# Low parts of the weights by TensorE, T~ of 64 tokens, two halves of attention by turns, and x in two buffers

## The chip, the core and the metric

The kernel runs on one core of one Trainium2 chip. The metric is device time of one execution in microseconds. Before the change it is 740.63 us, the median of three runs (740.49 to 740.67).

## The reference

Four batches of eight heads with 768 tokens and 48 columns a head go through a delta rule, and its output, 3072 rows of 384, through a layer of 2048 columns with the Mish function. The weights come as float64.

```python
k_n = k / (np.linalg.norm(k, axis=-1, keepdims=True) + 1e-06)
for t in range(S):
    kt, vt, bt = (k_n[:, :, t], v[:, :, t], beta[:, :, t, None])
    y[:, :, t] = np.einsum('bhd,bhde->bhe', q[:, :, t], state)
    v_old = np.einsum('bhde,bhd->bhe', state, kt)
    state = state + bt[:, :, :, None] * np.einsum('bhd,bhe->bhde', kt, vt - v_old)
...
h = x @ w_in
sp = np.where(h > 20.0, h, np.log1p(np.exp(np.minimum(h, 20.0))))
g = h * np.tanh(sp)
return (g @ w_out).astype(np.float32)
```

## The kernel before

**Chunks.** The tokens are taken in twelve chunks of 64. With G the strictly lower part of K K^T, V' the scaled values and b' the scaled beta, a chunk has Z = (I + G b')^-1 (V' − K S), Z~ = b' Z, S <- S + K^T Z~ and Y = Q S + lower(Q K^T) Z~. The matrix T~ = b' (I + G b')^-1 depends on no state, so it is made ahead, for a group of two chunks at a time (`early`, L205): two pg products a chunk (L235) give the Gram blocks, DVE turns them so that each partition holds one 32 x 32 block, and a forward substitution of 30 steps of two operations (L290, L295) inverts them. Each chunk has two blocks of 32 to a head, c = 0 and c = 1, so T~ is known only inside a block. For group 0 the substitution runs on blocks of 16, with 14 steps, and `merge` (L310) adds the missing quarter by products ma and mb on PE (L321, L333). For group 1 GpSimd takes steps 1 to 17. The first block's T~ parts end in the tile tu (L304) and tt (L301).

**A chunk's attention** (`step`, L355) works on four pieces, one batch each, tile `xx` holding for each head Z~, Q^T with the masked products of Q and K, and K or the identity, beside S. A piece has 8 products in each of five stages: gq (L381, K S and K Q^T), za (L398, Z~ of the first 32 tokens), pr (L413, what these do to the next 32, which DVE subtracts from `vt` in L419), zb (L398, the next 32) and py with ps (L431, L437, Y and the new S). ACT copies za, zb, py and ps out of PSUM. The stages of different batches are staggered, and 20 such steps a chunk are spread over the layer's pieces of the chunk before. All of attention's PSUM tiles share four banks (pool `pa`, tag "at").

**The layer** (`moe`, L487) takes the 256 rows of one chunk, turned by xt (L481) into x, high and low part (L483, L484), one buffer each. Float32 accuracy comes from three float32r products: high by high, high by low, low by high. Eight times: `h` (L505, 18 products of 256 columns into one of two PSUM buffers), ACT Exp (L509), DVE (L510), ACT Square, Ln, Exp (L511 to L513), DVE (L514, the tile e), ACT copies the high part of g (L522), DVE, or GpSimd in the first three chunks, subtracts for the low part (L525). Two `h` later `acc` (L535, 12 products of 384 columns) adds to the output tile.

**The weights** (`convert`, L171) come in 12 parts of w_in, 128 x 512 (tiles mi, wi), and 16 of w_out, 128 x 384 (mo, wo). A part is made float32 from the two words of float64: ACT's Abs (L179), DVE's clamp (L180), shift (L182), sign (L187) and low word (L189). For the first four parts ACT and GpSimd make the sign instead (L193). Then ACT copies the high part (L198) and GpSimd subtracts it for the low part (L199). Twelve of the parts are loaded among the other first loads, the rest from about one and a half chunks' time before the first layer on.

**Order.** Every piece of work is given a time in units of a chunk (`put`), and pieces are emitted in that order; the order on each engine is then a scheduler's, except that DVE keeps the order of what passes `queue` (L158). Products of zeros, `keep_warm` (L567), follow some attention products at the start.

Of the kernel before, what the change touches and what calls it, by code (L numbers as in the profile page):

```python
# [1 line left out]

# [31 lines left out]
def kernel(  # L34
# [36 lines left out]
    PB = NP // B  # L71
# [283 lines left out]
    def step(n, y):  # L355
# [8 lines left out]
        def s1(b, half=None):  # L364
# [3 lines left out]
            if n:  # L368
                scale_v(b)
# [369 lines left out]
```

## Time and profile before

| | |
|---|---|
| median of the runs | 740.63 us |
| span of the profiled execution | 745.6 us |
| instructions | 22768 |
| TensorE busy (PE) | 682.3 us, 92% of the span |
| VectorE (DVE) | 534.3 us, 72% |
| ScalarE (ACT) | 468.9 us, 63% |
| GpSimd (POOL) | 127.4 us, 17% |
| chain that ended last | PE 67%, DVE 20% |

The times of the runs are measured without the profiler, the span with it; the profiled execution's own time is its span. PE is a product's time, PEld the loading of its stationary operand, which runs beside other products. In a group's row stand the line, the engine, the operation, the tiles it writes and reads, shapes and count, then the busy time, the mean time of one in ns, and the engine's idle time just before, with what ended it. In a timeline's row stand start, duration, engine, line, operation, tiles, shapes, count, and the idle time before. A product of float32 has two records, one of float32r one.

### The profile page before, as it was taken

How to read it: one execution, taken by the hardware profiler on the slowest of the kernel's cores; microseconds unless marked ns; L12 is line 12 of the kernel's file. 1: busy time of each engine (PE TensorE's matmuls, PEld its weight loads, DVE VectorE, ACT ScalarE, POOL GpSimd, SP SyncE). 2: the span in 40 equal slices, each digit the busy share in tenths (PEclk: the TensorE clock that was granted, in tenths of full speed). 3: DMA queues.
4: the chain of work that ended last, by engine and by line, in shares of the span. 5: the costliest groups of instructions: out<-in, count | busy, mean ns of one | idle time of the engine just before them, and what ended most of it. 6: DMA issues, size and time to landing. Idle time of an engine off the chain costs nothing.

```text
span 745.6 us, 22768 instructions
## 1 busy us (share of the span) xinstructions
PE 682.3 (92%) x9656; PEld 602.3 (81%) x9674; DVE 534.3 (72%) x1152; ACT 468.9 (63%) x1005; POOL 127.4 (17%) x171
## 2 busy tenths in 40 slices
PE   5659699878799989999999999999999999999993
PEld 3236588768788878998898998998988989989993
DVE  5796999997747997659995579975499964454351
ACT  2233667755485666776776767767767767767681
POOL 3431336894221221000000000000000000000000
PEclk9756999789899999999999999999999999999998
DMA  5762910253213032122222221130130120000000
GB/s 87 185 181 40 380 32 7 30 84 60 25 32 59 8 54 48 21 44 50 37 34 41 40 38 34 24 51 15 24 59 14 33 49 18 18 23 1 17 7 21
DMA packets 160981, 37.75 MB, mean 51 GB/s; under 512 B 154224, under 2 KB 157296, under 8 KB 160880
## 3 DMA queue, kind: packets, MB, share of 16 engines
q1 hardware_dynamic: 160880, 36.30, 24.0%
q8 instruction: 76, 1.25, 0.7%
q14 instruction: 25, 0.20, 0.1%
HBM read 31.56 MB, written 4.72 MB: 49 GB/s over the span
## 4 chain that ended last, share of the span: by engine, by line
PE 67%; DVE 20%; SPq 4%; issue 3%; ACT 2%; DMA 2%; POOL 1%; DVEq 0%; POOLq 0%; ACTq 0%
PE h L505 24%; PE acc L535 22%; PE gq L381 4%; SPq L131 3%; PE py L431 3%; PE pg L235 2%; PE za L398 2%; DVE pr L290 2%; PE zb L398 2%; PE pr L413 2%; DVE gt L295 2%; PE warm L570 2%; PE ps L437 2%; DVE e L514 1%; DVE xx L389 1%
## 5 line engine op out<-in xcount | busy, mean ns | idle before, releaser
L505 PE MATMUL h<-x,wi 128*128 128x256 f32 x1728 | 238.3, 291 | 13.5 <-DVE e L514 12.1
L505 PEld LDWEIGHTS h<-x,wi 128*128 128x128 f32 x1728 | 218.4, 192 | 23.8 <-DVE e L514 12.5
L535 PE MATMUL acc<-wo,g 128*128 128x384 f32 x1152 | 233.4, 350 | 2.3 <-ACT g L522 1.9
L535 PEld LDWEIGHTS acc<-wo,g 128*128 128x128 f32 x1152 | 201.1, 192 | 8.8 <-ACT g L522 2.5
L514 DVE SCALAR_TENSOR_TENSOR e<-e,h 128x512 f32<-128x512 f32 x96 | 65.8, 685 | 45.5 <-ACT e L513 43.9
L522 ACT CAST g<-e 128x512 fp32r<-128x512 f32 x96 | 59.3, 618 | 49.6 <-DVE e L514 48.6
L361 POOL TENSOR_TENSOR vt<-vt,ne 128x192 f32<-128x192 f32 x48 | 27.3, 589 | 351.9 <-DMA vt<-in_v_dram 187.1
L509 ACT ACTIVATE e<-h 128x512 f32<-128x512 f32 x96 | 57.2, 596 | 47.9 <-PE h L505 45.2
L511 ACT ACTIVATE e<-e 128x512 f32<-128x512 f32 x96 | 60.5, 631 | 33.0 <-DVE e L510 32.5
L510 DVE TENSOR_SCALAR e<-e 128x512 f32<-128x512 f32 x96 | 42.7, 446 | 32.2 <-ACT e L509 31.0
L525 DVE TENSOR_TENSOR g<-e,g 128x512 fp32r<-128x512 f32 x72 | 49.1, 681 | 19.2 <-ACT g L522 18.6
L512 ACT ACTIVATE e<-e 128x512 f32<-128x512 f32 x96 | 60.5, 632 | 2.7
L513 ACT ACTIVATE e<-e 128x512 f32<-128x512 f32 x96 | 60.4, 631 | 2.4
L419 DVE TENSOR_TENSOR vt<-vt,pr 32x192 f32<-32x192 f32 x96 | 34.0, 354 | 32.7 <-PE pr L413 30.9
L290 DVE TENSOR_TENSOR pr<-gt 128x228 f32<-128x228 f32 (+14 forms) x147 | 53.9, 367 | 3.6 <-PE warm L292 0.5
L295 DVE TENSOR_TENSOR gt<-gt,pr 128x228 f32<-128x228 f32 (+14 forms) x147 | 51.5, 350 | 3.3
L372 DVE STREAM_TRANSPOSE xx<-qsrc 64x256 f32<-64x256 f32 x96 | 41.6, 437 | 13.9 <-PE ps L437 9.3
L381 PE MATMUL gq<-xx,kt 64*64 64x112 f32 (+1 forms) x768 | 47.6, 265 | 1.0 <-DVE x L484 1.0
L431 PEld LDWEIGHTS py<-xx 128*64 128x64 f32 x768 | 38.5, 138 | 10.7 <-issue 4.9
L431 PE MATMUL py<-xx 128*64 128x48 f32 x768 | 45.7, 227 | 1.0 <-ACT xx L403 0.3
L525 POOL TENSOR_TENSOR g<-e,g 128x512 fp32r<-128x512 f32 x24 | 31.9, 1328 | 74.1 <-ACT g L522 47.3
L381 PEld LDWEIGHTS gq<-xx,kt 64*64 64x64 f32 x768 | 37.4, 138 | 8.4 <-issue 4.5
(94 smaller groups left out, 838.3 us busy)
## 6 DMA issues: line engine op xcount, KB each, us to landing
ri<-in_moe_w_in_dram SPq DMA_DIRECT2D x12, 512.0 KB
ro<-in_moe_w_out_dram SPq DMA_DIRECT2D x16, 384.0 KB
vt<-in_v_dram SPq DMA_DIRECT2D x48, 96.0 KB
xx<-in_k_dram SPq DMA_DIRECT2D x96, 48.0 KB
out_dram<-o SPq DMA_DIRECT2D x24, 192.0 KB
qsrc<-in_q_dram SPq DMA_DIRECT2D x48, 64.0 KB
ksrc<-in_k_dram SPq DMA_DIRECT2D x44, 64.0 KB
qsrc<-in_q_dram SPq DMA_DIRECT2D x48, 32.0 KB
```

The lines of the kernel that those rows point to most:

```text
L290: queue(eng.tensor_tensor(out=pv, in0=nj, in1=xj, op=ALU.mult), on)
L295: queue(eng.tensor_tensor(out=below, in0=below, in1=pv, op=ALU.add), on)
L381: m = nc.tensor.matmul(ps[64 * hh:64 * hh + 64, p, :], kt[r, PB * b + p], x[r, p, hh, D - d:D + C], start=True, stop=True)
L431: nc.tensor.matmul(py[64 * hh:64 * hh + 64, p, :], x[:, p, hh, D:D + C], x[:, p, hh, 0:D], start=True, stop=True)
L505: nc.tensor.matmul(h[:, f2, :], wt["i", f * P // WI * NCH + c][:, i2, f0:f0 + P], x[:, c, :], start=(i == 0), stop=(i == 3 * NCH - 1))
L511: nc.scalar.activation(e, e, AF.Square)
L512: nc.scalar.activation(e, e, AF.Ln, bias=0.5, scale=0.5)
L513: nc.scalar.activation(e, e, AF.Exp, scale=-1.0)
L514: nc.vector.scalar_tensor_tensor(e, e, -1.0, h, op0=ALU.add, op1=ALU.mult)
L522: nc.scalar.copy(out=gg[:, 0], in_=e)
L525: eng.tensor_tensor(out=gg[:, 1], in0=e, in1=gg[:, 0], op=ALU.subtract)
L535: nc.tensor.matmul(acc[t], gg[:, a, f2, ts_], wt["o", f][:, i2, :], start=(f == 0 and i == 0), stop=(f == NF - 1 and i == 2))
```

## The change

The same numbers are computed, with this done in another way:

- **Halves.** A pair of heads that shares instructions is now (batch b, batch b+2), so a chunk's attention has two halves of 8 pairs instead of four pieces of 4, and `xx` two tiles.
- **T~ of 64 tokens.** The tile tt2 has 64 columns. After the blocks of 32 are done, ta = (masked K K^T of the two blocks) T~ and tb = T~ ta (functions s_a and s_b, 32 products of 32 columns each) fill the square between them. GpSimd copies the upper diagonal block beside it (move_diagonal), and DVE makes tn, the turned T~, that tb needs. Then one product of 64 rows a head, pz, gives all of Z~: za, pr, the subtraction and zb are gone.
- **By turns.** `together` emits the products of two stages alternately: pz of half 0 with gq of half 1, pz of half 1 with gq of the next chunk's half 0, tb of one chunk with ta of the next. gq is two tiles of four pairs a half. A half's py and ps stand alone. So a chunk's attention stands at four places in the layer.
- **Group 1** is split in 16s too, with merges 2 and 3; GpSimd's steps of the substitution are gone.
- **Weights.** Signs are all made by DVE. The low part of the first 22 parts is had on PE: a product with the identity of the float32 weight, plus one of its high part, into a tile lo of the attention's banks, which ACT copies with a minus sign. The stored number a is the weight's negative, so the high part is copied with a minus sign too. The last six low parts are DVE's. All parts are asked for at the start, among the other loads. 22 of the 28 parts have their conversion ahead of the first layer's `h`.
- **Order.** From t = −0.05 on (just ahead of the first `h`) PE keeps the order in which things are emitted. `h` and `acc` of all chunks form one sequence, so the next chunk's first two `h` stand before this chunk's last two `acc`. x has two buffers, and the turn of x stands before the last `h` of the chunk before. The last chunk's g takes a buffer of tn as well.
- **Keep-warm.** Behind each half of a merge stand 4 units of 128 columns instead of 18; behind each of chunk 0's other stages, 8.

```diff
-    PB = NP // B
+    PB = NP // 2
...
-    xx = [cp.tile([P, PB, 2, W], F32, name=f"xx{i}") for i in range(B)]
+    xx = [cp.tile([P, PB, 2, W], F32, name=f"xx{i}") for i in range(2)]
...
+    tt2 = cp.tile([P, 2, NP, C], F32, name="tt2")
...
-        if not rest:
-            sg = high.bitcast(F32)
-            nc.scalar.activation(sg, sg, AF.Sign, scale=-1.0)
-            nc.gpsimd.tensor_tensor(out=a, in0=a, in1=sg, op=ALU.mult)
...
-            nc.scalar.copy(out=w[:, 0], in_=a)
-        nc.gpsimd.tensor_tensor(out=w[:, 1], in0=a, in1=w[:, 0], op=ALU.subtract)
+        nc.scalar.mul(out=w[:, 0], in_=a, mul=-1.0)
+        if parts.index((kind, i)) < TN['pl']:
+            ps = pa.tile([P, 512], F32, tag="at", name=f"lo{kind}{i}")[:, :n]
+            nc.tensor.matmul(ps, ident, a, start=True, stop=False)
+            nc.tensor.matmul(ps, ident, w[:, 0].bitcast(F32), start=False, stop=True)
+            nc.scalar.mul(out=w[:, 1], in_=ps, mul=-1.0)
+            queue(nc.vector.scalar_tensor_tensor(w[:, 1], a, -1.0, w[:, 0], op0=ALU.mult, op1=ALU.subtract))
...
+    def move_diagonal(t2):
+        for hh in range(2):
+            r = slice(64 * hh, 64 * hh + 32)
+            nc.gpsimd.tensor_copy(out=tt2[r, t2, :, 0:32], in_=tt2[r, t2, :, 32:])
...
+    def together(*stages):
+        for step in zip_longest(*stages):
+            for f in step:
+                if f is not None:
+                    f()
...
+    def s_a(n):
+        at, tt = ats[n], tt2[:, n % 2]
+        ps = pa.tile([P, NP, 32], F32, tag="at", name=f"ta{n}")
...
+                r = slice(64 * hh + 32, 64 * hh + 64)
+                yield mm(ps[64 * hh:64 * hh + 32, p, :], at[r, p, :], tt[r, p, 32:],
+                         then=out if p == NP - 1 and hh else None)
...
+    def s_z(n, h):
+        vt, x, tt = vts[n, h], xx[h], tt2[:, n % 2]
+        pz = pa.tile([P, PB, D], F32, tag="at", name=f"pz{n}_{h}")
...
+                yield mm(pz[r, p, :], tt[r, PB * h + p, :], vt[r, p, :], then=out if p == PB - 1 and hh else None)
...
-        xs = [mp.tile([P, NCH, UT], F32R, tag=f"x{i}", name=f"x{i}_{n}", bufs=1) for i in range(2)]
+        xs = [mp.tile([P, NCH, UT], F32R, tag=f"x{i}", name=f"x{i}_{n}", bufs=2) for i in range(2)]
...
+    for n in range(1, NS):
+        t = n - 1.1 / NFP
+        put(one(turn, n), 1, t, t)
...
+        at(ts[0], (s_z, n, 0), (s_gq, n, 1))
+        at(ts[1], (s_y, n, 0))
+        at(ts[2], (s_z, n, 1), (s_gq, n + 1, 0))
+        at(ts[3], (s_y, n, 1))
...
+        at(t0 + u[0], (s_a, n))
+        at(t0 + u[1], (s_b, n), (s_a, n + 1))
+        at(t0 + u[2], (s_b, n + 1))
...
-    m0, m1 = TN.get('m', (9, 9))
+    m0, m1 = TN['m0'], 99
```

How this moves PE's instructions in a steady chunk. Before, in the layer of chunk 6 between two of its pieces (`x2` is that many alike in a row; a name's second number is the chunk's piece or batch, its last a buffer's): py and ps of one batch end, an `acc` follows, then zb of one batch, pr of the next.

```order
L437 MATMUL ps_0_6692<-xx_98 48x48 x2
L431 MATMUL py_0_6691<-xx_98 64x48 x2
L437 MATMUL ps_0_6692<-xx_98 48x48 x2
L535 MATMUL acc_6_6389<-wo_1102,g_2_6521 128x384 x3
L535 MATMUL acc_6_6389<-wo_1203,g_2_6521 128x384 x3
L535 MATMUL acc_6_6390<-wo_1102,g_2_6521 128x384 x3
L535 MATMUL acc_6_6390<-wo_1203,g_2_6521 128x384 x3
L398 MATMUL zb_1_6730<-vt_0_6192,tt_5497 32x48 x8
L413 MATMUL pr_2_6744<-xx_100,at_4402 32x48 x8
L505 MATMUL h_5_6755<-x_6_6280,wi_1462 128x256
```

Each stage of a batch is a piece of its own, zb and pr of neighbours standing together. Now, in the layer of chunk 5, the first rows of the place behind its fifth `h`: pz of half 1 and gq of the next chunk's half 0, one product of each in turn.

```order
L528 MATMUL h_4_6058<-x_5_5558,wi_1322 128x256
L393 MATMUL pz_1_6089<-vt_1_5024,tt_106 64x48
L393 MATMUL gq_00_6093<-xx_98,kt_4292 64x112
L393 MATMUL pz_1_6089<-vt_1_5024,tt_106 64x48
L393 MATMUL gq_00_6093<-xx_98,kt_4292 64x112
L393 MATMUL pz_1_6089<-vt_1_5024,tt_106 64x48
L393 MATMUL gq_00_6093<-xx_98,kt_4292 64x112
```

The two stages that stood at places of their own, with layer pieces between, are now one piece of 32 products, and its tiles are of one size.

The start on PE, now: merge 0 with low parts of w_out beside it.

```order
L335 MATMUL ma_0_572<-tu_564,d_156 32x16 x32
L583 LDWEIGHTS zero
L583 MATMUL warm<-zero 128x512
L335 MATMUL ma_1_608<-tu_564,d_156 32x16 x32
L583 LDWEIGHTS zero
L583 MATMUL warm<-zero 128x512
L199 MATMUL loo_646<-mo_568,ident 128x384
L200 MATMUL loo_646<-wo_644,ident 128x384
L199 MATMUL loo_658<-mo_650,ident 128x384
L347 MATMUL mb_0_667<-tt_106,ym_566 32x16 x14
L200 MATMUL loo_658<-wo_656,ident 128x384
L347 MATMUL mb_0_667<-tt_106,ym_566 32x16 x18
```

Before, the place holds ma and mb with five warm products behind each half and no low part. On GpSimd, before, behind the scaling of v (L361):

```order
L361 TENSOR_TENSOR vt_1_327<-vt_1_327,ne_397 128x192 x2
L193 TENSOR_TENSOR mi_402<-mi_402,ri_151 128x512
L199 TENSOR_TENSOR wi_418<-mi_402,wi_418 128x512
L193 TENSOR_TENSOR mi_473<-mi_473,ri_330 128x512
L199 TENSOR_TENSOR wi_490<-mi_473,wi_490 128x512
```

And now at the same place:

```order
L374 TENSOR_TENSOR vt_1_322<-vt_1_322,ne_420 128x384
L313 MEMSET ym_566 128x32x16
L323 COPY tt_106<-tt_106 32x16x32 x2
L374 TENSOR_TENSOR vt_0_976<-vt_0_976,ne_420 128x384
L374 TENSOR_TENSOR vt_1_979<-vt_1_979,ne_420 128x384
```

The conversion has left GpSimd; four short copies of diagonal blocks a group have come.

More of the change, by code (lines that the diff above doesn't have):

```diff
@@ new lines, in mm, with run, out @@
+    def mm(*a, then=None):
+        def run():
+            last[:] = [nc.tensor.matmul(*a, start=True, stop=True)]
+            if then is not None:
+                then()
+        return run
+    def s_a(n):
+        at, tt = ats[n], tt2[:, n % 2]
+        ps = pa.tile([P, NP, 32], F32, tag="at", name=f"ta{n}")
+        def out():
+            for hh in range(2):
+                r = slice(64 * hh, 64 * hh + 32)
+                nc.scalar.mul(out=at[r], in_=ps[r], mul=-1.0)
+        for p in range(NP):
+            for hh in range(2):
+                r = slice(64 * hh + 32, 64 * hh + 64)
+                yield mm(ps[64 * hh:64 * hh + 32, p, :], at[r, p, :], tt[r, p, 32:],
+                         then=out if p == NP - 1 and hh else None)
@@ new lines, in s_b, with out @@
+    def s_b(n):
+        at, tt, tn = ats[n], tt2[:, n % 2], tns[n // 2]
+        ps = pa.tile([P, NP, 32], F32, tag="at", name=f"tb{n}")
+        def out():
+            for hh in range(2):
+                r = slice(64 * hh, 64 * hh + 32)
+                nc.scalar.copy(out=tt[r, :, 32:], in_=ps[r])
+        for p in range(NP):
+            for hh in range(2):
+                r = slice(64 * hh, 64 * hh + 32)
+                yield mm(ps[r, p, :], tn[r, n % 2, p, :], at[r, p, :], then=out if p == NP - 1 and hh else None)
@@ L642, with at, run @@
     put(one(loads, TN.get('d1', ["q", "v", 2, "k2", 2, "k3", 2, "x", 22])), 1, -2.901, -2.901)
-    put(attend0, 1, -2.3, -2.3)
+    def at(t, *stages, warm=0):
+        def run():
+            together(*(f(*a) for f, *a in stages if a[0] < NS))
+            keep_warm(warm, last[-1])
+            yield
+        put(run(), 1, t, t)
+    put(one(lambda: [scale_v(0, h) for h in range(2)]), 1, -2.3, -2.3)
     put(one(loads, TN.get('d2', [28])), 1, TN.get('p1', -1.2) + 0.001, TN.get('p1', -1.2) + 0.001)
@@ L673 @@
             put(gen, 1, t, t)
[L674 to L685 removed]
+    units = [moe(n) for n in range(NS)]
@@ new lines @@
+    todo1 = [(n, fp) for n in range(NS) for fp in range(NFP)]
+    todo2 = list(todo1)
+    t = 0.0
+    lag = 2
+    for k, (n, fp) in enumerate(todo1):
+        t = n + (fp + 0.25) / NFP
+        put(one(units[n][0], fp), 1, t, t)
+        if n == NS - 1 and fp == 2:
+            lag = 3
+        elif k >= lag:
+            m, fq = todo2.pop(0)
+            t = n + (fp + 0.75) / NFP
+            put(one(units[m][1], fq), 1, t, t)
+    for i, (m, fq) in enumerate(todo2):
+        put(one(units[m][1], fq), 1, NS + i, NS + i)
```

322 lines of the change are left out of this document (132 added, 190 removed).

## The prediction

> **What bounds the kernel now.** I read the profile in this order: the page's head and slices, then busy time by stage (the span cut where the first `h` starts and where each chunk's output copies end), then groups of instructions, then single stretches of the timeline. The page first: the span, the granted clock in 40 slices, and the costliest group.
>
> ```profile
> span 745.6 us, 22768 instructions
> ...
> PEclk9756999789899999999999999999999999999998
> ...
> L505 PE MATMUL h<-x,wi 128*128 128x256 f32 x1728 | 238.3, 291 | 13.5 <-DVE e L514 12.1
> ```
>
> The profiled execution's 745.6 us stand 5.0 above the median of 740.63; I sum against 745.6 and take 5.0 off at the end. A slice is 18.6 us: the clock is under .9 in the first eleven slices only. By stage (the start from T~0's merges to the first `h`; chunk 0; 1; 2; 3 and 4; 9; 10; 11; the tail):
>
> ```profile
> core 0: us, PE busy (x) PEld busy (x) DVE busy (x) ACT busy (x) POOL busy (x), PEclk, DMA share, GB/s
> 44.00:93.10 49.10, 40.66 (x948) 27.25 (x959) 39.72 (x77) 21.04 (x56) 14.48 (x15) 0.71 0.64 215
> 93.10:176.10 83.00, 72.14 (x994) 65.06 (x993) 79.99 (x144) 54.44 (x117) 55.77 (x65) 0.89 0.27 40
> 176.10:228.40 52.30, 46.12 (x718) 42.66 (x717) 28.08 (x59) 32.24 (x74) 11.49 (x10) 0.93 0.22 38
> 228.40:288.00 59.60, 55.10 (x741) 48.34 (x743) 55.59 (x123) 36.56 (x81) 13.95 (x15) 1.00 0.24 39
> 288.00:392.80 104.80, 104.53 (x1526) 94.97 (x1526) 81.62 (x191) 73.37 (x159) 4.22 (x9) 1.00 0.24 40
> 602.20:651.40 49.20, 49.20 (x614) 44.86 (x612) 24.01 (x50) 35.65 (x76) 0.97 (x2) 1.00 0.14 27
> 651.40:700.50 49.10, 49.10 (x571) 44.55 (x570) 22.93 (x47) 33.91 (x70) 0.00 (x0) 1.00 0.03 9
> 700.50:734.30 33.80, 33.72 (x240) 33.40 (x238) 14.19 (x24) 24.05 (x43) 0.00 (x0) 1.00 0.04 13
> 734.30:745.60 11.30, 0.00 (x0) 0.00 (x0) 0.00 (x0) 0.45 (x1) 0.00 (x0) 0.73 0.10 35
> ```
>
> Chunk 0 is DVE's: 79.99 busy of 83.0. From 288 on PE never rests (104.53 of 104.8), so there only fewer or better packed products help. Chunks 1 and 2 lie between, PE idle 6.2 + 4.5 = 10.7. The last chunk has no attention beside it and gives the layer's bare price, by the groups in 700.5 to 734.3:
>
> ```profile
> L505 PE MATMUL h<-x,wi 128*128 128x256 f32 x144 | 17.8, 281 | 0.0
> L535 PE MATMUL acc<-wo,g 128*128 128x384 f32 x96 | 17.3, 334 | 0.0
> ```
>
> A chunk's layer is 33.8, an `h` 17.8 / 8 = 2.23, its products .124 each.
>
> **A steady chunk, part by part.** The pieces of attention as they stand between layer pieces, PE alone (records of a piece overlap, so a piece lasts from its start to the next one's):
>
> ```profile
> 517.54 0.98 PE L381 MATMUL gq<-xx,kt 64*64 64x112 f32 x16
> 518.46 2.41 PE L505 MATMUL h<-x,wi 128*128 128x256 f32 x18
> 520.80 0.32 PE L431 MATMUL py<-xx 128*64 128x48 f32 x4
> ...
> 521.76 2.38 PE L535 MATMUL acc<-wo,g 128*128 128x384 f32 x12
> 524.07 0.40 PE L398 MATMUL zb<-vt,tt 32*32 32x48 f32 x10
> ...
> 524.74 2.40 PE L505 MATMUL h<-x,wi 128*128 128x256 f32 x18
> 527.06 1.10 PE L235 MATMUL pg<-kt 64*32 64x64 f32 x64
> 528.09 0.53 PE L398 MATMUL za<-vt,tt 32*32 32x48 f32 x16
> 528.55 1.32 PE L535 MATMUL acc<-wo,g 128*128 128x384 f32 x6
> ```
>
> One batch: gq .92 (8 products, two records each), py with ps .96, za .46, zb with pr of another batch by turns .67, where apart they would be twice .46. Four batches: 3.68 + 3.84 + 1.84 + 2.68 = 12.04; two pg 2.06; layer 33.8. Chunks 3 and 4 took 104.8 / 2 = 52.4, so 4.5 is left for the transposes of x and for going from layer to attention and back at some 18 places. With .6 to .8 put to the transposes, about .21 a place.
>
> Now the change. Half a chunk has 16 gq products (1.84) and 16 pz by turns. Below: pz wholly inside gq, 1.84. Above: one after the other at za's price, 2.76, though a pz has 64 rows. By turns zb and pr take .67 / .92 = .73 of their sum, which gives 2.0; I take 2.1, nearest to that row. A chunk: 4.2 for gq, za, pr and zb together, before 8.2: −4.0. py and ps are the same products. New are ta and tb, 32 products of 32 columns each a chunk. By zb and pr's row, 16 products of 48 columns in .67, both are 1.34 × 2 × 32/48 = 1.8; alone at za's price 3.7; at best, with four tiles of 32 rows abreast all along, a quarter of that, .9. I take 1.8. The places fall from 18 to about 5.5 (four pieces, and ta, tb, pg, transposes mostly at the same places): −12.5 × .21 = −2.6. Sum −4.8: 47.6. DVE's and ACT's answers now come in fewer, larger lumps, an evicted piece being a whole half; I put .9 for it, and x's second buffer lets the next layer's first two `h` start before the last `acc`, which hides the turn of chunks. **48.5 a chunk**, 2.1 less where no pg is left.
>
> On DVE the subtractions behind pr go; the transposes for tn come. Both are off the path while PE is full.
>
> **The start.** T~0's merges start here, waiting for DVE, at half clock:
>
> ```profile
> 43.86 1.05 PE L321 MATMUL ma<-tu,d 16*32 16x16 f32 x64 [6.22 <-DVE tu L304]
> ```
>
> What GpSimd did to DVE in chunk 0, in rows of the timeline, of the groups in 93.1 to 176.1 and, for the least/median/longest, of the whole run; and GpSimd's own rows:
>
> ```profile
> 79.57 1.45 POOL L199 TENSOR_TENSOR wi<-mi,wi 128x512 fp32r<-128x512 f32 x1 [0.24 <-ACT wi L198]
> 79.83 1.46 DVE L182 TENSOR_SCALAR mi<-mi 128x512 int32<-128x512 int32 x1
> ```
> ```profile
> L187 DVE SCALAR_TENSOR_TENSOR mo<-ro,mo 128x384 int32<-128x384 int32 x9 | 9.0, 995 | 0.2
> L187 DVE SCALAR_TENSOR_TENSOR mi<-ri,mi 128x512 int32<-128x512 int32 x6 | 6.7, 1116 | 0.2
> L189 DVE SCALAR_TENSOR_TENSOR mo<-ro,mo 128x384 int32<-128x384 int32 x10 | 6.3, 633 | 0.2
> L189 DVE SCALAR_TENSOR_TENSOR mi<-ri,mi 128x512 int32<-128x512 int32 x6 | 5.4, 896 | 0.1
> ```
> ```profile
> L187 DVE SCALAR_TENSOR_TENSOR mo<-ro,mo x15: 508/830/1526, 46.6 to 170.2; 128x384 int32<-128x384 int32 x15
> L187 DVE SCALAR_TENSOR_TENSOR mi<-ri,mi x9: 639/694/1717, 67.4 to 144.9; 128x512 int32<-128x512 int32 x9
> ```
> ```profile
> L199 POOL TENSOR_TENSOR wo<-mo,wo 128x384 fp32r<-128x384 f32 x16 | 16.7, 1045 | 22.2 <-ACT wo L198 21.9 <-PE zb L398 0.3
> L199 POOL TENSOR_TENSOR wi<-mi,wi 128x512 fp32r<-128x512 f32 x12 | 16.6, 1380 | 29.2 <-ACT wi L198 26.4 <-DMA xx<-in_k_dram 2.8
> ```
>
> A sign operation without company takes .51 or .64, in chunk 0 it took 1.0 to 1.1: DVE waits while GpSimd works. L187 and L189 there sum to 27.4; at .51 and .64 they would be 19 × .51 + 12 × .64 = 17.4, so 10 are lost in these two, and about as much again, I estimate, in the other two lines and in the layer's: 17 to 20, at most the 33.3 that GpSimd's L199 lasts. The Trainium skill ("SBUF — State Buffer", section "Who interferes with whom") says that the one of DVE and GpSimd that comes second blocks fully when both want the shared port pair; the rows at 79.57 and 79.83, where DVE ends .27 behind GpSimd, agree. By that rule the regained time could be all 33.3, and chunk 0 below would be DVE-free earlier still; the sum keeps the measured excess.
>
> A low part by PE is two products of 512 or 384 columns of full float32. By gq's row, 8 × 112 columns in .92 with two abreast, a column costs 2.05 ns: 2.1 (i) and 1.58 (o). Below, by `h`'s .124 for 256 columns: .5 and .37; above, at half clock, 4.2 and 3.2. Between ma0 and `h0` PE now has ten o and six i low parts: 15.8 + 12.6 = 28.4. Beside them there: merges 0 and 1 at no more than 1.05, 8; ta, tb 2; gq, pz 3.7; py, ps 3.8; four pg 4.1; the rest of the warming products some 2: 52. Three more signs (and one o) ahead of it on DVE put ma0 at 45.5. So `h0` comes at 97.5 at full clock, at 45.5 + 52 / .71 = 118.7 at the old mean clock. DVE in that stretch: sixteen parts at four operations of at most .51 or .64, 20.4 + 15.4 = 35.8, the products' answers and group 1's first steps some 18: 99. I take **112**, 18.9 later than 93.1, nearer to the slow clock since PE still waits for its parts there.
>
> Chunk 0 then: DVE keeps six of the parts (4 × 2.0 + 2 × 2.6 = 13.2), with their low parts 3.3, group 1's split solve of 28 short steps at about .3 (8.4, at most 18), and what it had besides conversion: 79.99 less about 45 (27.4 and nearly as much for the other two lines at two thirds) leaves 35. Sum 60; g's low parts on GpSimd stay and are in the 35. PE: layer 33.8, two `h` of chunk 1 4.5, attention and merges some 18, over .89: 63. With 3 of waits **66**, for 83.0: −17, and two `h` of chunk 1 are done in it.
>
> Chunks 1 and 2: 2 × 48.5, and 5, half of the 10.7 idle, for waits: 102 for 111.9, −9.9. Chunks 3 to 8: from 288.0 to 602.2 now 314.2, then 6 × 48.5 − 2.1 = 288.9: −25.3. Chunk 9: no pg there, 49.2 − 4.0 − 2.6 + .5 + 1.9 for waits and late tb = 45: −4.2. Chunk 10: 49.1 − 4.0 − 2.6 − .9 (half its gq went ahead) = 41.5: −7.6. Chunk 11: two `h` are done, 33.8 − 4.5 + .7 = 30: −3.8. Tail the same 11.3. Altogether 18.9 − 17 − 9.9 − 25.3 − 4.2 − 7.6 − 3.8 = −48.9: 696.7 of span, less 5.0, **692 us**.
>
> What I cost at nothing: x's second buffer costs no engine time. SP issues k's loads into xx twice a chunk in larger pieces, behind py and ps as before, and q's and v's a chunk earlier, ahead of output stores; in chunks 3 and 4 the DMA engines are .24 busy, which hides them, and a load that came late would hold a half's gq or py by its own few us. Weights that are all asked for at the start arrive ahead of their conversions, which run until 170.2 now (L187). If that cover failed, `h0` would wait for w_in's first parts, not the last.
>
> **The rivals.** (1) DVE becomes the steady bound. It was busy 81.62 of 104.8 in chunks 3 and 4, keeps all but the subtractions behind pr after the edit, with two transposes a group added, and 97 is all that two chunks then give; the whole solve, 60 dependent operations, is to fit between turns 1.1 chunks apart, with the layer's operations queued among them. Against it: even 81.62 of 97 leaves 15. If it holds the layer's e, chunks 3 to 8 last 51.5 each (+18), chunks 1 and 2 108.5 (+6.5): 717. Chance .14.
>
> (2) The clock stays low at the start, since PE now stands in written order and a low part that isn't ready holds what is behind it, while 14 of the 18 units of 128 warming columns behind each half of a merge are gone. Then 52 / .58 = 90 and `h0` at 135: +23, 715. For it: .71 already. Chance .12.
>
> (3) Slower: `h` waits at its buffer. Two PSUM buffers of `h` go free by DVE's e (L514), 12.1 of the 13.5 idle before `h` came from there, nearly all in the start. Before, a piece of attention stood at most of the gaps and covered that chain; with four lumps a chunk several `h` follow with only an `acc` between, and in written order PE cannot take anything else. An `h` and an `acc` make 2.23 + 2.16 = 4.4 us, and the chain holds two Exp, Square, Ln and two DVE operations. In the last chunk now, with no attention, there is no idle before `h` (0.0 above), which speaks against it, but there DVE has nothing else. At .8 for each of 8 × 10 `h` this is +64: 756. It decides from 48.6 / 80 = .6 an `h`. Chance .10.
>
> That the change doesn't do what it says: the low parts of six pieces stay on DVE, and the turns might not pack: then gq with pz cost 2.76 and ta, tb 3.7 a chunk, +3.2 × 10 = +32, 724; it is in the range.
>
> **How the numbers follow.** The forecast has .62, and its own range by its unknown prices is 673 to 712 (`h0` 14 earlier or 7 later; 48.5 less .5 or plus 1.3 over ten chunks). Rivals 1 and 2 lie at 715 to 717, packing at 724, both of the first two at 740. A range of 668 to 728 leaves out the slower rival (.10) and some .04 on either side. A measurement here tells .2%, 1.5 us, from no change. Faster .88, same .02, slower .10.
>
> **What would show it.** Right: output copies some 48 to 49 us apart from chunk 3 on with PE still never idle; the first `h` near 112 and the end of chunk 0 near 178; L187 at .51 and .64 throughout; a pair of gq and pz within 2.0 to 2.2. Rival 1 shows as PE idle before `acc` or `h` released by DVE e, in solve chunks only; rival 2 as a granted clock under .65 between 45 and 110; rival 3 as idle before every second `h` in all chunks. Wrong would be: a chunk over 52 with PE full, so that the turns cost more than the stages they replace, or a low part of PE over 3 us at full clock.

## The result and the profile after

The changed kernel takes 727.74 us, median of four runs (726.80 to 730.24), against 740.56 in four runs of the kernel before: a ratio of 0.983, 95% interval 0.981 to 0.985. It is 1.7% faster, by 12.8 us where 48.6 were forecast. The head of its page, span and granted clock:

```profile
span 726.0 us, 23400 instructions
...
PEclk9696998997999999999999999999989999999998
```

The span is 1.7 below the median here, where the span before lay 5.0 above its median: 6.7 of the error is that offset, which is no property of a kernel and which I carried over. Every execution whose span is on record took 1.7 to 2.5 longer than its span (727.98 for 726.0 here); by that the profiled execution of the kernel before lasted at least 747.3 (an estimate), so it was itself a long one, some 7 above the median. The rest is in the span, forecast at 696.7. By stage, in the columns of the stages before: from ma0 to the first product of `h`; to the rest of that `h`; to the second `h`; to chunk 0's end; chunk 2; chunks 3 and 4; 7 and 8; 10.

```profile
50.40:105.20 54.80, 44.60 (x832) 27.24 (x845) 37.20 (x74) 28.06 (x55) 3.41 (x5) 0.84 0.53 162
105.20:123.10 17.90, 14.45 (x402) 9.57 (x404) 10.89 (x22) 5.81 (x15) 1.21 (x2) 0.81 0.18 29
123.10:136.10 13.00, 9.14 (x124) 6.10 (x122) 12.82 (x35) 7.95 (x17) 3.14 (x5) 1.00 0.00 1
136.10:209.60 73.50, 63.76 (x1490) 59.52 (x1487) 47.51 (x105) 44.11 (x85) 13.65 (x13) 0.93 0.18 26
266.50:311.50 45.00, 44.67 (x732) 42.97 (x722) 26.44 (x41) 33.63 (x63) 12.27 (x12) 1.00 0.26 45
311.50:362.80 51.30, 47.05 (x695) 45.71 (x694) 45.96 (x111) 32.01 (x61) 2.87 (x4) 0.97 0.25 42
362.80:408.60 45.80, 45.80 (x815) 44.52 (x815) 30.59 (x53) 34.08 (x63) 3.66 (x5) 1.00 0.25 45
504.80:558.90 54.10, 47.95 (x696) 46.61 (x695) 47.57 (x116) 31.56 (x60) 3.09 (x4) 0.94 0.16 31
558.90:604.10 45.20, 45.06 (x696) 43.72 (x695) 26.59 (x45) 33.82 (x62) 3.66 (x5) 1.00 0.17 33
647.60:686.00 38.40, 38.40 (x344) 37.80 (x343) 15.38 (x26) 27.11 (x50) 0.00 (x0) 1.00 0.03 12
```

From 311.5 to 604.1 six chunks take 292.6, 48.8 each against 48.5 forecast, and all from chunk 0's end to the end of the span 726.0 − 209.6 = 516.4 against 518.7. So the sum behind chunk 0 came out. Chunk 0's end did not: 209.6 against 178, where the profile of before had 176.1. The start and chunk 0 gave back 33 of the 53 us that the rest gained.

A pair of pz and gq in a steady chunk, first row and the row behind it:

```profile
352.92 0.25 PE L393 MATMUL pz<-vt,tt 64*64 64x48 f32 x1
...
354.62 2.38 PE L562 MATMUL acc<-wo,g 128*128 128x384 f32 x12
```

It lasts 1.70, below the 1.84 that I had set as the least, gq alone. That bound was two pieces of 8 products; run 5 below has 16 gq products in one piece, in at most 1.68 (from 356.84, their first record, to 358.52). So by turns the 32 products take about what gq takes alone there: pz is nearly free.

One wait is new in every second chunk, PE at the turn of x. The waits of PE in chunks 3 to 8:

```profile
engine line waited for: us in total, times, longest us
PE xt L503 <- ACT yy L485: 13.2, 3, 6.2
PE pg L239 <- issue: 0.7, 1, 0.7
```

And one at the start, on DVE, between 20 and 50 us:

```profile
DVE mo L186 <- ACT mo L185: 6.3, 1, 6.3
DVE mi L186 <- ACT mi L185: 2.7, 1, 2.7
DVE pr L294 <- PE warm L296: 1.7, 1, 1.7
```

DVE stops 6.3 us in the middle of group 0's substitution for ACT's Abs of the first w_out part. What ACT waits for is in its own row, and what PE does then in its rows:

```profile
43.88 0.55 ACT L185 ACTIVATE mo<-ro 128x384 f32<-128x384 f32 x1 [5.45 <-PE loi L199]
```
```profile
31.70 11.23 PE L583 MATMUL warm<-zero 128*128 128x512 bf16 x45
42.77 1.02 PE L199 MATMUL loi<-mi,ident 128*128 128x512 f32 x2
```

ACT has no buffer for the new part, because an older one is still to be read by PE's low-part product, and that product stands behind the batch of 46 warming products (11.2 us). Before the change nobody read that buffer from PE. The conversion's sign operation is no longer stretched, as its least, median and longest show:

```profile
L190 DVE SCALAR_TENSOR_TENSOR mo<-ro,mo x16: 490/557/559, 45.5 to 161.9; 128x384 int32<-128x384 int32 x16
L190 DVE SCALAR_TENSOR_TENSOR mi<-ri,mi x12: 651/687/693, 23.8 to 139.2; 128x512 int32<-128x512 int32 x12
```

### The profile page after: what moved, and what is told of

Read it like the earlier page. It is cut to its first block, busy times and chain, and to the rows that moved or that the text cites. A ratio compares the mean times of both kernels' runs of the same rounds, so it can differ in the third digit from the quotient of the medians.

```text
span 726.0 us, 23400 instructions
## 1 busy us (share of the span) xinstructions
PE 649.3 (89%) x10219; PEld 589.0 (81%) x10238; DVE 488.0 (67%) x1029; ACT 438.8 (60%) x815; POOL 81.9 (11%) x108
## 4 chain that ended last, share of the span: by engine, by line
PE 58%; DVE 21%; ACT 7%; SPq 5%; issue 4%; DMA 3%; POOL 0%; DVEq 0%; ACTq 0%; POOLq 0%
PE h L528 21%; PE acc L562 19%; SPq L137 5%; DVE pr L294 3%; DVE gt L299 3%; PE gq L393 3%; DVE e L537 2%; PE py L393 2%; PE warm L583 2%; DVE xx L444 2%; DMA ri<-in_moe_w_in_dram 1%; DVE gt L250 1%; PE ta L393 1%; ACT e L534 1%; PE ps L393 1%
## 5 line engine op out<-in xcount | busy, mean ns | idle before, releaser
L528 PE MATMUL h<-x,wi 128*128 128x256 f32 x1728 | 229.2, 288 | 0.9 <-DVE e L537 0.9
L528 PEld LDWEIGHTS h<-x,wi 128*128 128x128 f32 x1728 | 221.9, 193 | 2.8 <-PE acc L562 0.9
L562 PE MATMUL acc<-wo,g 128*128 128x384 f32 x1152 | 223.0, 342 | 1.2 <-ACT e L534 1.1
L537 DVE SCALAR_TENSOR_TENSOR e<-e,h 128x512 f32<-128x512 f32 x96 | 65.7, 685 | 89.1 <-ACT e L536 88.4
L532 ACT ACTIVATE e<-h 128x512 f32<-128x512 f32 x96 | 57.0, 594 | 53.3 <-PE h L528 49.3
L533 DVE TENSOR_SCALAR e<-e 128x512 f32<-128x512 f32 x96 | 43.8, 456 | 44.2 <-ACT e L532 43.8
L294 DVE TENSOR_TENSOR pr<-gt 128x84 f32<-128x84 f32 (+14 forms) x148 | 53.6, 362 | 4.8 <-PE warm L296 1.7
L299 DVE TENSOR_TENSOR gt<-gt,pr 128x84 f32<-128x84 f32 (+14 forms) x148 | 49.6, 335 | 3.1
L374 POOL TENSOR_TENSOR vt<-vt,ne 128x384 f32<-128x384 f32 x24 | 21.7, 904 | 219.1 <-DVE ne L284 94.6
L444 DVE TENSOR_TENSOR xx<-gq,amask 64x256 f32<-64x256 f32 x96 | 40.2, 418 | 6.3 <-PE gq L393 5.6
L550 POOL TENSOR_TENSOR g<-e,g 128x512 fp32r<-128x512 f32 x24 | 31.8, 1327 | 105.2 <-ACT g L547 70.5
L393 PE MATMUL gq<-xx,kt 64*64 64x112 f32 (+1 forms) x768 | 42.1, 256 | 0.8 <-ACT xx L484 0.7
L393 PE MATMUL py<-xx 128*64 128x48 f32 x768 | 41.3, 224 | 0.0
L393 PE MATMUL ps<-xx 128*48 128x48 f32 x704 | 37.4, 208 | 0.0
```

What stands on the lines that cost most here:

```text
L294: queue(eng.tensor_tensor(out=pv, in0=nj, in1=xj, op=ALU.mult), on)
L299: queue(eng.tensor_tensor(out=below, in0=below, in1=pv, op=ALU.add), on)
L393: last[:] = [nc.tensor.matmul(*a, start=True, stop=True)]
L528: nc.tensor.matmul(h[:, f2, :], wt["i", f * P // WI * NCH + c][:, i2, f0:f0 + P], x[:, c, :], start=(i == 0), stop=(i == 3 * NCH - 1))
L532: nc.scalar.activation(e, h, AF.Exp, scale=-1.0)
L537: nc.vector.scalar_tensor_tensor(e, e, -1.0, h, op0=ALU.add, op1=ALU.mult)
```

## The experiments

Each runs against the kernel before on the same chip (740.3 to 741.6 in all sets); behind a time stands its ratio to that kernel, with the 95% interval. "Base" is the changed kernel, measured once, in the result above; most later runs start from run 1. A stage's end comes from one profile a run. Runs 1, 6 and 16, which are alike in all that stands up to chunk 0's end, end it at 196.3, 200.4 and 194.9, so a difference of some 5 us there says little by itself.

**1. Fewer warming products in the substitution.**

```diff
-jt=5,wt=46
+jt=5,wt=16
```

> 16 warming products of 512 columns instead of 46 behind the fifth step of group 0's substitution. Theory A (the batch of 46, 11.2 us on PE, holds the second low part behind it; the tile of the float32 weight is not given back, so ACT's next Abs waits, and DVE, which keeps its queue's order, stands for 6.3 us in the middle of the substitution): the first ma product comes at 44 to 45 us instead of 50.4, DVE's wait of 6.3 is under 1, chunk 0 ends 5 to 6 us earlier than at 209.6, and the time falls from 727.7 to about 722. Rival B (the warming products earn their place by the clock): ma comes earlier too, but the granted clock between 44 and 105 falls from .84 to under .75, and chunk 0's end and the time stay within 2 us.

718.14 us, ratio 0.969 (0.967 to 0.972). ma comes at 43.6, 6.8 earlier, and chunk 0 ends at 196.3, 13.3 earlier, more than twice what was expected. The other 6.5 come between ma and the first whole `h` (109.9 instead of 123.2), and were not traced. DVE's waits in the same stretch:

```profile
DVE pr L294 <- PE warm L296: 1.4, 1, 1.4
DVE mi L186 <- ACT mi L185: 0.6, 1, 0.6
DVE rc L264 <- ACT y L261: 0.6, 1, 0.6
```

The wait of 6.3 is gone, as theory A has it, and rival B is out: the clock in 44 to 105 rose, from .86 to .89.

**2 and 3. The low parts by DVE, or by GpSimd, instead of PE** (46 warming products, as in the base).

```diff
-pl=22
+pl=0
```

> All 28 low parts by DVE, none by PE: 44 products leave PE (some 40 us of it at full clock before and in chunk 0), 22 operations of .55 to .69 come to DVE (13 us). Theory A (the start is long because PE carries the low parts in front of the layer's first products, in written order): ma at 44 to 46, the first whole h before 112 instead of 123, chunk 0's end at 195 to 200 instead of 209.6, time 713 to 718. Rival C (DVE bounds the start, and PE's low parts fill idle time): chunk 0's end at 218 to 223, time 737 to 742.

```diff
-        nc.scalar.mul(out=w[:, 0], in_=a, mul=-1.0)
...
+        nc.scalar.copy(out=w[:, 0], in_=a)
+        nc.gpsimd.tensor_tensor(out=w[:, 1], in0=a, in1=w[:, 0], op=ALU.subtract)
...
-            nc.scalar.activation(e, h, AF.Exp, scale=-1.0)
+            nc.scalar.activation(e, h, AF.Exp)
```

> All 28 low parts by GpSimd as before the change, all else changed; weights negative as before. Theory A: PE's 40 us go as in the run with DVE, but DVE's conversion operations stretch again (sign of w_out from .55 to about 1.0 on average), so chunk 0 ends between 200 and 212 and the time lies at 718 to 730, a few us above the run with all low parts on DVE. Rival E (GpSimd's company costs more than PE's products, as the change supposes): chunk 0's end after 215, time over 733.

720.61 (0.972, 0.970 to 0.975) by DVE and 720.37 (0.972, 0.970 to 0.974) by GpSimd. Both are 7 us better than the base. By DVE chunk 0 ends at 207.2, between the two theories' ranges, and the time lies above A's. By GpSimd it ends at 200.2: theory A's ranges hold and rival E is out, so as the change stands GpSimd's company costs less than PE's low parts do. PE has its products off, but it rests more, and its clock falls. The stretch 44 to 105 in run 1, then in run 2:

```profile
44.00:105.00 61.00, 53.74 (x1085) 32.13 (x1075) 44.63 (x87) 31.42 (x63) 4.46 (x7) 0.89 0.62 172
```
```profile
44.00:105.00 61.00, 42.90 (x1075) 30.92 (x1073) 50.42 (x97) 24.98 (x49) 5.34 (x7) 0.66 0.61 168
```

In run 3 the clock there is .70. Without low parts on PE none of them stands behind the 46 warming products, so DVE's wait of 6.3 is gone here too (ma at 47.9 and 44.8), and run 1 is the nearer comparison: there PE's low parts win by 2.5 and 2.2 us. The low parts on DVE or GpSimd together with 16 warming products were not run.

Run 2 also shows what then holds chunk 0. Its first whole `h` comes at 97.7, 12.2 ahead of run 1's, but from there to chunk 0's end it takes 109.5 instead of 86.4. The stretch 97 to 160 there:

```profile
97.00:160.00 63.00, 38.38 (x795) 35.70 (x798) 60.67 (x137) 33.49 (x64) 11.91 (x13) 0.80 0.11 17
```

DVE is busy 60.67 of 63.0.

**4. Chunk 0 in the scheduler's order.**

```diff
-m0=-0.05
+m0=1
```

> PE keeps the written order only from chunk 1 on instead of just ahead of the first h; chunk 0's order is the scheduler's. Rival D (the written order makes PE wait in chunk 0: 12.9 us idle between 123 and 209.6): idle there falls to under 6, chunk 0's end to about 201, time 718 to 721. Theory A (products, not order): chunk 0's end within 3 us of 209.6, time 725 to 731.

726.56 (0.981, 0.978 to 0.984), 1.2 below the base, with intervals that overlap. Chunk 0's end comes at 204.2, 5.4 earlier and between the two theories' ranges, and PE rests 8.9 instead of 13.6 in it; chunks 3 to 8 take 298.4 instead of 292.6 and give that back. Rival D explains at most 5 of the 31 us by which chunk 0 ended late.

**5. No turns.** The products of each stage are emitted one stage after the other.

```diff
-        for step in zip_longest(*stages):
-            for f in step:
-                if f is not None:
-                    f()
+        for stage in stages:
+            for f in stage:
+                f()
```

> The changed kernel (46 warming products) with the products of two stages one stage after the other instead of by turns. Theory A (by turns the two stages share PE's tiles, as the sum had it, 2.1 to 2.3 for a pair against 2.76): each pair of pz and gq costs .4 to .6 more, tb with ta .3, together 1.0 to 1.5 a chunk, so chunks 3 to 8 average 49.8 to 50.3 instead of 48.8, and the time is 739 to 744. Rival F (turns give nothing, fewer places and fewer stages gave the chunk's 3.7): chunk 3 to 8 average within .3 of 48.8, time 726 to 731.

744.51 (1.003, 1.001 to 1.005), 16.8 above the base, .3% slower than before the change. A pair of pz and gq, without company:

```profile
356.09 0.96 PE L392 MATMUL pz<-vt,tt 64*64 64x48 f32 x26
356.84 0.31 PE L392 MATMUL gq<-xx,kt 64*64 64x112 f32 x2
...
357.08 1.51 PE L392 MATMUL gq<-xx,kt 64*64 64x112 f32 x28
358.52 2.38 PE L561 MATMUL acc<-wo,g 128*128 128x384 f32 x12
```

2.43 against 1.70. Two pairs a chunk make 1.46; tb with the next chunk's ta, once in two chunks, takes 2.05 (398.75 to 400.80) instead of 1.21 (191.26 to 192.47 in the base), another .4. That covers the 1.7 by which the chunks grew: chunks 3 to 8 average 50.5 instead of 48.8. Theory A holds, by somewhat more than it was put at, and rival F is out. Without the turns the changed kernel would be no faster than the one before.

**6. A wider substitution** (from run 1).

```diff
-        put(gen, 63, t0 - 2.6, t0 - 1.5)
-        put(gen, 1, t0 - 1.43, t0 - 1.43)
+        put(gen, 63, t0 - 2.68, t0 - 1.3)
+        put(gen, 1, t0 - 1.26, t0 - 1.26)
```

> With 16 warming products as in the first run; in addition a group's substitution is spread over 1.38 chunks instead of 1.1, and its last step comes .17 of a chunk later. Theory G (in the chunk that holds the substitution DVE's queue makes e wait up to 4.6, ACT behind it copies Y late, PE waits 4.3 for the turn of x and then runs at half clock for some us: 51 to 55 against 45 in the other chunk): the long chunks of 3 to 8 fall from 51.3 to 54.7 to about 48.5, the short ones rise by under 1, the sum over 3 to 8 falls by 8 to 10, time 708 to 711. Rival H (PE's own products make the long chunk long, four pg stand in it): no change, 716 to 720.

720.25 (0.969, 0.964 to 0.974), the ratio of run 1. Chunks 3 to 8 did not move (49.3 on average in both), and it is no test: the order on DVE is the scheduler's, and it put the steps in the same places within a chunk.

**7. Fewer parts ahead of the first `h`** (from run 1).

```diff
-(-1.0,16),(-0.05,22),(0.35,28)]
+(-1.0,14),(-0.05,17),(0.55,28)]
```

> With 16 warming products; in addition 17 instead of 22 parts of the weights are converted ahead of the first h, the rest up to .55 of chunk 0. Theory A (in written order the low parts of parts that are needed late stand ahead of the first two h on PE and wait there for DVE): the first whole h comes 6 to 10 us earlier than at 109.9 and the second at 108 to 114 instead of 122.8; chunk 0's end falls by 4 to 8 from 196.3, time 710 to 714. Rival I (the work of chunk 0 on DVE and PE is the same whenever it comes): first h earlier, but chunk 0's end within 2 of 196.3, time 716 to 720.

715.39 (0.963, 0.959 to 0.967). The second `h` comes at 118.0 instead of 122.8, but the first whole one only at 109.1, and chunk 0's end, 197.5, does not move. The time fell by 2.7; its profile has that in chunks 3 to 8 (293.1 against 295.7), which the edit does not touch. For chunk 0 this favours rival I, though the time lies just under I's range.

**8. Merges 2 and 3 later** (from run 1).

```diff
-m2=(0.6,0.66),m3=(0.68,0.74)
-u1=(0.8,0.92,1.35)
+m2=(0.7,0.76),m3=(0.82,0.88)
+u1=(0.9,1.0,1.35)
```

> With 16 warming products; in addition merges 2 and 3 and the ta of chunk 2 stand about .1 of a chunk later on PE. Theory A (PE stands about 6 us in front of merge 2, where written order puts it before DVE has ended group 1's substitution): these waits fall under 2, chunk 0's end from 196.3 to 190 to 193, time 712 to 715. Rival J (DVE is the bound there, and what PE gains it loses at the next h): chunk 0's end within 1.5, or chunk 1 longer by as much, time 717 to 719.

718.18 (0.966, 0.961 to 0.971): no gain. Chunk 0 ends at 197.0; PE's wait for DVE ahead of the merge is gone, and 4.4 come at the mb behind it, for ACT. Rival J's ranges hold.

**9 and 10. The turn of x behind the last `h`**, from run 1, and with run 7's edit.

```diff
-        t = n - 1.1 / NFP
+        t = n - 0.5 / NFP
```

> With 16 warming products; in addition the turn of x stands behind the last h of a chunk on PE instead of ahead of it. Theory G (in a substitution's chunk Y comes late out of ACT, PE stands up to 6.6 at the turn of x, 17.9 in four chunks, and comes back at a lower clock): the waits at xt fall by 2.3 each or more, long chunks by 2 to 4, short ones unchanged, time 706 to 712 instead of 718.1. Rival H (the products themselves make the long chunk long): periods unchanged, 716 to 720; rival L (the next chunk's first h then waits for x): the short chunks lengthen by 1 to 2, time 718 to 726.

> 16 warming products, 17 parts ahead of the first h and the turn of x behind the last h, together. If the three effects add: 718.1 less 2.7 (late parts) less 6 to 10 (turn): 704 to 711, and faster than both kernels. If the turn does nothing: 714 to 717.

742.20 (1.002, 0.999 to 1.005) and 743.42 (1.001, 0.997 to 1.005). Rival L, three times as large as it was put: run 9 is 24 us slower than run 1. The wait at xt, 13.6 in chunks 3 to 8 of run 1, is gone, but now, in the same chunks of run 9, `h` waits for x and for e:

```profile
PE h L528 <- ACT x L505: 8.0, 4, 2.2
PE h L528 <- DVE e L537: 6.0, 3, 2.2
PE h L528 <- DVE x L506: 4.7, 5, 1.4
```

The short chunks go from 45 to 47 up to 48 to 52. So the early turn is worth 24 us in the whole run. The waits explain a part only: 18.7 in place of 13.6, where chunks 3 to 8 grew by 12.5 and chunk 0 ended 9.4 later (4.3 of that ahead of the first whole `h`). What makes up the rest was not traced.

**11. All low parts by DVE, and more warming.**

```diff
-pl=22
+pl=0
...
-wmg=4
+wmg=18
...
-warm=8)
+warm=24)
```

> All low parts by DVE, none by PE, and the warming products that PE then lacks: 18 units behind a merge and 24 behind each stage of chunk 0, 46 products in the substitution. Theory A (a low part's price on PE is what the start pays, and the run with low parts on DVE, 720.6, only lost that gain to a clock of .66 between 44 and 105): clock there over .8, chunk 0's end at 193 to 198 instead of 207.2, time 708 to 714. Rival K (with the clock held the place of the low parts is worth nothing, since warming products take PE's time as low parts do): clock over .8, but chunk 0's end at 203 to 209 and time 717 to 723.

722.31 (0.975, 0.971 to 0.979). The clock of the stretch is .80, up from .66, and chunk 0 still ends at 205.3: rival K's numbers, and the clock alone did not cost run 2 its gain. K's reason is not what the trace shows, though: the warming products do not fill the low parts' place ahead of the first `h`, since the first whole `h` comes at 99.7, 10.2 ahead of run 1's. The time is lost behind it, where DVE is full, as in run 2:

```profile
97.00:160.00 63.00, 44.60 (x804) 40.55 (x804) 60.12 (x141) 33.76 (x64) 9.97 (x11) 0.80 0.09 15
```

So runs 2 and 11 tell what the low parts cost on DVE, and not what they are worth on PE alone; run 15 does that.

**12. One buffer of x.**

```diff
-name=f"x{i}_{n}", bufs=2)
+name=f"x{i}_{n}", bufs=1)
```

> The changed kernel with 46 warming products and one buffer of x. Theory A (the second buffer lets the next chunk's x be written before the last h have read this one): ACT's and DVE's writes of x wait for the last h, whose place on PE is behind xt: PE stands 2 to 4 us in each chunk at the next h, +25 to +45, time 752 to 772. Rival M (written order has an acc in between, which covers it): under +6, time 727 to 734.

736.80 (0.995, 0.992 to 0.997), 9.1 above the base, between the two theories. Theory A's wait is not there: in chunks 3 to 8 PE never waits at `h` for x, and in the whole of the chunks up to 8 it does so once, for 1.2. The early turn of x can stand with one buffer too. Of the 7.5 that the span grew, 3.7 lie before chunk 0's end and 2.6 in chunks 3 to 8; where the one buffer costs them was not traced.

**13. Y earlier** (from run 7).

```diff
-else (0.05, 0.3, 0.55, 0.8))]
+else (0.05, 0.28, 0.5, 0.7))]
```

> 16 warming products and 17 parts ahead of the first h, as in the run of 715.4; in addition, from chunk 2 on, the second half's pz and py/ps stand about a twentieth and a tenth of a chunk earlier, so that one more h and acc lie between py/ps and the turn of x. Theory G (Y leaves ACT late in a substitution's chunk, 17.9 of waits at xt in four chunks): waits at xt under 6, long chunks 47 to 50 instead of 51 to 54, time 704 to 709. Rival H (the products make the long chunk long): 713 to 717. Rival N (the same wait then comes at py/ps for Z~): 712 to 720 with PE idle at py or pz.

710.51 (0.960, 0.957 to 0.962), the best version, faster than both kernels and 1.5 above theory G's range. PE's waits from chunk 1 to chunk 8:

```profile
PE h L528 <- DVE e L537: 4.9, 6, 1.1
PE xt L503 <- ACT yy L485: 4.3, 1, 4.3
PE pz L393 <- ACT tt L422: 1.4, 5, 0.6
```

The long chunks of 3 to 8 fall from 51.4, 52.0 and 53.9 to 48.9, 48.7 and 49.6, the short ones end at 44.7 to 46.7. Theory G holds: rivals H and N are out.

**14, 15, 16. Three prices by leaving work out** (all from run 1).

```diff
+        if g:
+            for h8 in range(2):
+                yield
...
+            return
```

> 16 warming products; merges 2 and 3 leave out their products, so that T~ of chunks 2 and 3 lacks a quarter of its lower part. Theory A (chunk 0 is long by PE work that the sum left out, the merges of group 1 among it, 7 us with 6 of waits): chunk 0's end from 196.3 to 184 to 190, time 706 to 712. Rival C (DVE and ACT hold chunk 0): chunk 0's end within 3 us, time 715 to 719.

```diff
-            nc.tensor.matmul(ps, ident, a, start=True, stop=False)
-            nc.tensor.matmul(ps, ident, w[:, 0].bitcast(F32), start=False, stop=True)
-            nc.scalar.mul(out=w[:, 1], in_=ps, mul=-1.0)
+            nc.scalar.mul(out=w[:, 1], in_=a, mul=-1.0)
```

> 16 warming products; the 22 low parts leave out their products on PE, ACT writes a copy in their place. It measures the price of PE's low parts alone. Theory A (they take 40 us of PE, of which the part ahead of the first h and in chunk 0 is on the path): chunk 0's end from 196.3 to 176 to 186, time 698 to 708. Rival K (they fill time in which PE waits, and hold the clock): chunk 0's end 190 to 198, time 712 to 720, and a granted clock between 44 and 105 under .8.

```diff
+            if g > 1 and j > 15:
+                yield
+                yield
+                continue
```

> 16 warming products; from group 2 on the substitution does 15 of 30 steps. It measures what DVE's substitution costs the steady chunks. Theory G: the long chunks of 3 to 8 fall from 51.3, 52.5, 54.7 to 46 to 49, short ones unchanged, time 706 to 711. Rival H: periods within .5, time 716 to 720.

Without group 1's merges 710.86 (0.961, 0.957 to 0.965), chunk 0's end 190.9, 5.4 earlier: theory A, within a us. Without PE's low parts 711.05 (0.961, 0.958 to 0.963), chunk 0's end 187.3, 9.0 earlier, between the two theories, and the clock as rival K had it. The 22 low parts are ten of w_in and twelve of w_out; at 1.72 and 1.44 each (twice .86 and twice .72 from start to start in PE's rows) they take 34.5, less than the 40 that were put. Two things go with getting back only 9. The clock falls:

```profile
44.00:105.00 61.00, 47.22 (x1277) 35.20 (x1270) 54.38 (x108) 38.81 (x79) 5.21 (x6) 0.69 0.65 180
```

And PE, without them, waits 10.9 at ma for DVE and 7.8 at tb for ACT, where run 1 waits 4.3 and nothing. How much each of the two is worth was not separated.

With half of the substitution 719.14 (0.972, 0.970 to 0.975): no change in time. Two of the three long chunks fall to 49.7 and 49.0, two of the short ones rise to 47.9 and 47.8, and PE's waits at xt in chunks 3 to 8 are the same three:

```profile
PE xt L507 <- ACT yy L489: 13.8, 3, 7.2
PE pg L239 <- issue: 1.6, 2, 0.8
```

So halving what the substitution has DVE do does not take the waits away, and moving Y away from the turn does (run 13): theory G holds in its place and not in its amount.

## Why the prediction was right or wrong

**In short.** Against the forecast's span of 696.7 the kernel has 726.0. The first whole `h` came 11.2 late, chunk 0 took 20.4 longer than its 66, and all behind it 2.3 less than forecast; the 6.7 of the offset come on top. The steps that failed are two: what stands ahead of the first `h`, where a low part's buffer was left out, and chunk 0's sum, where PE's work beside the layer was put at 18 and is 27.8, and its waits at 3 and are 13.6.

**The steady chunk: right, by terms that partly cancel.** 48.8 against 48.5. The pair of gq and pz was put at 2.1 and is 1.70, so 3.4 a chunk instead of 4.2. The waits were put at .9 and are larger: 13.2 at xt in six chunks, 2.2 a chunk, and a clock of .94 to .97 in the long chunks. Some luck is in how near the sum came. The waits lie in the substitution's chunks, as rival 1 had them, but its mark, PE idle before `acc` or `h` for DVE's e, was not found: PE stands at xt for ACT's copy of Y, which comes behind the layer's operations on ACT, and of these a Square has waited 4.56 for DVE's part of e:

```profile
338.93 0.63 ACT L534 ACTIVATE e<-e 128x512 f32<-128x512 f32 x1 [4.56 <-DVE e L533]
344.01 0.46 ACT L485 COPY yy<-py 128x384 f32<-128x384 f32 x1
344.53 0.86 PE L503 MATMUL xt<-ident,yy 128*128 128x128 f32 x3 [4.25 <-ACT yy L485]
```

So DVE did get in the way, at one place in two chunks, and it did not hold the layer.

**The transitions and the end: right in the main.** Chunk 10 took 38.4 against 41.5, chunk 9 43.5 against 45, chunk 11 29.6 against 30. Chunks 1 and 2 took 56.9 + 45.0 = 101.9 against 102; their sum was forecast, the long and the short one were not.

**ma0: wrong.** I had it at 45.5, for more signs on DVE; it came at 50.4. What I did not look for is the way back: a low part on PE holds a buffer of the conversion until PE reads it, PE stood behind 46 warming products, and ACT and DVE's fixed queue stood with it. Run 1 undoes just that and ma0 comes at 43.6, no later than before the change (43.86), so the price that I put on the signs does not show either.

**The first `h`: wrong by the same.** Put at 112, its first product stood alone at 105.2 and the other seventeen at 123.2. With 16 warming products they come at 109.9, so the 46 cost 13.3 here, more than the whole error of 11.2. The price of a low part was put too high, 2.1 worked out, 42.77 to 44.49 in PE's rows, 1.72, at full clock. That the stretch would run at .71 was wrong too: it was .84, and .89 in run 1. By the sum both bring `h` earlier than 112, so that run 1 still lands near it is partly luck.

**Chunk 0: wrong, the largest term.** Put at 66, it took 209.6 − 123.2 = 86.4, and 86.4 again in run 1, so the batch of 46 has no part in it. The forecast set DVE's 60 beside PE's 63, took the larger and added 3 for waits. DVE's sum was right: it is busy 60.3. PE's was not: it is busy 9.14 + 63.76 = 72.9, of it 45.1 with the layer (43 forecast at the clock of .89). All else is 27.8, where "attention and merges some 18" make 20 at that clock. And PE rests 13.6, where I wrote 3. The two groups of the layer between 123.1 and 209.6:

```profile
L528 PE MATMUL h<-x,wi 128*128 128x256 f32 x185 | 26.3, 299 | 0.6 <-DVE e L537 0.6
L562 PE MATMUL acc<-wo,g 128*128 128x384 f32 x96 | 18.8, 344 | 0.0
```

The 27.8 hold group 1's four merge stages a chunk, three chunks' ta, the last low parts and the next group's pg, which I had not counted one by one. Run 14 puts the merges, with their waits, at 5.4, run 15 all low parts, those ahead of the first `h` too, at 9.0.

Behind the 13.6 in which PE rests stands the overlap, which the sum took for granted: the larger of two sums is the time only if both engines find work all through. In the trace the chunk falls into a part in which DVE is full and two in which it is not. Below the three stretches stand the longest of PE's waits.

```profile
123.10:163.00 39.90, 32.77 (x487) 27.62 (x485) 39.42 (x100) 26.81 (x52) 8.75 (x9) 1.00 0.11 17
163.00:176.00 13.00, 9.49 (x374) 9.06 (x376) 7.68 (x15) 4.57 (x11) 2.99 (x4) 0.61 0.02 5
176.00:209.60 33.60, 30.64 (x756) 28.93 (x753) 13.23 (x25) 20.68 (x40) 5.04 (x5) 1.00 0.26 37
```
```profile
PE loi L199 <- DVE pr L294: 3.0, 1, 3.0
PE ma L335 <- DVE tu L310: 2.3, 1, 2.3
PE mb L347 <- POOL ym L313: 1.9, 1, 1.9
PE pg L239 <- DVE kt L220: 1.6, 1, 1.6
```

Up to 163 DVE is busy 39.42 of 39.9, with the last parts, group 1's substitution and the layer's e, while PE rests 7.1. When DVE is through, 40.1 of PE's work are still to come, and they take 46.6, from 163 to 176 at a clock of .61. Of PE's 13.3 of waits in the chunk 8.3 end by DVE. The moment at which DVE has turned group 1's blocks (tu, ended at 163.4 here) goes with the chunk's end: that comes 46.2 later here, and 45.7 to 46.4 later in runs 1, 3, 4, 6 and 16, where tu ends anywhere between 148.8 and 157.8; 40.0 later in run 14, which has no merges of group 1 behind it. In the other runs, most of which change something around that moment (no turns, the last parts later, low parts on DVE, the turn of x), it is 44.2 to 61.1 later. This is read from the traces; no run took work off DVE in this stretch alone, so that DVE sets the chunk's end is argued and not shown. Order (run 4), fewer parts ahead (run 7) and later merges (run 8) left the chunk from its first whole `h` at 82.6, 88.4 and 88.9, near its 86.4.

**DVE's relief: right in kind, and worth little.** The sign of a w_out part takes .557 in the middle and .559 at the longest, of a w_in part .687 and .693, where before it took .830 and .694 in the middle and up to 1.526 and 1.717; the forecast's .51 and .64 were the least seen. By the rule of the Trainium skill that I weighed ("SBUF — State Buffer", "Who interferes with whom") up to all of GpSimd's time would come back. Run 3 gives the company back: DVE's sign stretches again, up to 1.34 and 1.76. Yet run 3 ends only 2.2 us behind run 1 and 7.4 ahead of the base. Why the relief is worth so little is not shown. Ahead of the first whole `h` DVE is not the busier of the two: between 50.4 and 123.1 it is busy 48.1 and PE 59.1.

**The rivals.** Rival 2 is out: the clock of that stretch was higher than before, not lower. Rival 3 is out: `h` waited .9 for e in the whole run. That turns might not pack was the rival to fear: run 5 shows that without them the change would be no gain at all.

## What to carry to other kernels

Work that moves to an engine also moves its buffers behind that engine's queue: before it is priced, look at what stands ahead of it there, warming products too, and who needs the buffer next. Two stages of the same tile shape, emitted by turns, can take little more than the longer of them alone (1.70 for the pair; one stage after the other 2.43, of which gq at most 1.68). And where two engines are both nearly full, the larger of their sums is a floor and no forecast: look whether the work of the one is over before the other's can start. Here DVE's 60 and PE's 73 made 86.

## What the runs showed of the hardware

Float32 products on 64 x 64 tiles by turns: 32 products of 48 and 112 columns in 1.70, one stage after the other 2.43. Real work keeps the clock as warming products do: with PE's low parts the granted clock in 44 to 105 was .89 (run 1), without them .66 to .70 (runs 2, 3 and 15), with more warming products in their place .80 (run 11). Leaving out 34.5 us of products moved chunk 0's end by 9.0 (run 15), with the clock at .69 there and PE waiting longer for DVE and ACT.
